# A spectral filter beside a product-key expert layer on one core: score columns laid key by key, expert flags weighted on ScalarE, and the written-out order renewed

## The chip, the cores and the metric

One core of one Trainium2 chip runs the whole kernel. The metric is the device time of one execution in microseconds (us), the median of several runs. TensorE (PE; its weight loads are shown apart as PEld), VectorE (DVE), ScalarE (ACT), GpSimd (POOL) and SyncE (SP, which here only starts DMAs) run beside each other and wait for each other through semaphores.

## The reference

```python
def _A_ref(x, w_r, w_i):                 # a filter in the 2-D Fourier domain
    X = rfft2(x) * (w_r + 1j * w_i)      # x: 1 x 2048 x 576
    return irfft2(X, s=(2048, 576))

def _B_ref(x, w_q, k1, k2, u, v):        # 32 heads, 8 + 8 keys, 64 experts, top 1
    q = einsum("nd,dhc->nhc", xf, w_q)
    s1 = einsum("nhd,ed->nhe", q[..., :128], k1)
    s2 = einsum("nhd,ed->nhe", q[..., 128:], k2)
    e = argmax(s1) * 8 + argmax(s2)      # per token and head
    act = gelu(einsum("nd,nhd->nh", xf, u[e]))
    return sum_over_heads(act * v[e])    # softmax over one candidate is 1

xn = layernorm(x)                        # no affine part
return x + _A_ref(xn, w_r, w_i) + _B_ref(xn, w_q, k1, k2, u, v)
```

## The kernel before, in words

**Filter.** `ln` and `folds` normalise 16 tiles of 128 rows and fold the 576 columns by their symmetries (sums and differences, shared between DVE and POOL). The mean is taken out in the folds: POOL makes `rr[:, 2] = -4*mean`, and a DVE scalar_tensor_tensor adds it into the even fold. `dft128` multiplies a folded tile by a 64-point transform, whose weights `Rs` ACT scales by the row's 1/sigma; ACT and DVE evict the product into `AF_`/`AB` (and `ABL`, its 33 left-over columns). For three tiles (`RTS`) the product is made in two half-height matmuls per block. `d_fwd(g)` does the transform along the columns, `s_fwd` the rest of the one along the rows, `s_mul` multiplies with the filter (DVE reads the product from PSUM as `banks`, writes `t`; POOL combines into `y`; ACT and POOL split it into two float16 halves `yh`), `s_inv(g)` transforms back (16 of them, evicted by ACT and DVE into `AB` and `ABL`). When all 16 are in, `d_inv(t)` does the last transform per tile; ACT and DVE (and POOL for the even tiles) make `qs`/`yh` and `eo`/`t` of it, multiplying by the scale `sc[:, 12]`, POOL makes `y`/`A`, and `fin(t)` multiplies by `RT`, adds the experts' part (`CAT` times `vS`) in the same PSUM tile, DVE adds x, and two DMAs write the result.

**Experts.** `fold_part` contracts the query weights (32 loads `w<-in_wq_dram` of 576 KB) with the seven key differences per side, `fold_end` and `fold_last` turn and split them into `MU`, 448 score columns that ACT and DVE write as (64 sides and heads, 7 keys), with 64 columns for u behind them. `x_t(r)` makes the two float16 halves of x transposed (`xT`): two ACT passes and one POOL subtraction each, 16 in all. `scores(r)`, r = 0 to 7, multiplies two tiles: 28 matmuls of 512 columns. ACT makes gelu, DVE the maximum `mx` over the seven keys, the flags `eq` (buffer `w`), and their product with the weights `wt`. `route(r)` reduces the weighted flags and builds the index words with a chain of DVE steps (scratch in `MT`), `combine(r)` reduces them, turns them to int32 (two tensor_scalar), masks with `fm`, multiplies by `sc[:, 9]` and the activation, and PE turns the result into `CAT`.

**Order.** The program is recorded first. `_Plan.forward` then plays the recorded operations through five engine queues with the costs of `_Plan.cost`; among those that are ready it takes the one with the lowest number in `RANK`, a table with a number for each operation. The order in which it takes them is the order in which the instructions are issued; PSUM tiles are given out in the same pass (`LIMIT`: two tiles at a time for scores, four banks for each of the kinds a, b, c). All recorded instructions carry the line of one call in `issue`, L523.

Of the kernel before, what the change touches and what calls it, by code (L numbers as in the profile page):

```python
# [196 lines left out]
)  # L197
# [1054 lines left out]
```

## Time and profile before

| | before |
|---|---|
| median of 3 runs | 222.97 us (222.16 to 223.46) |
| the profiled execution | 221.33 us, its span 219.5 us |
| granted TensorE clock | 0.995 |
| PE / PEld busy | 193.5 us (88%) / 130.7 us |
| DVE busy | 178.0 us (81%) |
| ACT / POOL busy | 132.5 us (60%) / 134.1 us (61%) |
| DMA | 48.12 MB |

Busy time is per engine, as a share of the span. An engine can be busy all the time in one stage and idle in another, so the stages are looked at one by one below. The profiled execution is 1.83 us longer than its span and 1.64 us under the median.

### The profile page before, as it was taken

To read this page: it belongs to the slowest core of one execution; us is meant where nothing else is said; L and a number is where in the kernel's file an instruction comes from. 1 tells how busy PE (TensorE), PEld (TensorE's weight loads), DVE (VectorE), ACT (ScalarE), POOL (GpSimd) and SP (SyncE) were. 2 spreads that over 40 slices of the span, in tenths; PEclk is the share of its full clock that TensorE was granted. 3 is DMA by queue.
4 is the path that set the end of the run, shared out by engine and by line. 5 is a ranking of instruction groups with operands and counts; after the bars stand their busy time and mean duration, and the time that the engine had idled before them with its cause. 6 is when DMAs were issued, how large, how long until landed. Compare 5 with 4: busy or idle time off the path is not lost.

```text
span 219.5 us, 6058 instructions
## 1 busy us (share of the span) xinstructions
PE 193.5 (88%) x2360; PEld 130.7 (60%) x2360; DVE 178.0 (81%) x417; ACT 132.5 (60%) x285; POOL 134.1 (61%) x179
## 2 busy tenths in 40 slices
PE   0197899999999989999989999999979999998690
PEld 0175576679568546764657545655547787477560
DVE  1989899854646777763999999998899999999980
ACT  2268787979946977988595983855832333043220
POOL 4776787515189307394767963947734985667560
PEclk9999999999999999999999999999999999999998
DMA  6999999999999999993362404201100136204376
GB/s 198 380 417 418 422 418 423 395 403 400 366 383 356 405 408 423 437 345 133 103 199 63 131 0 122 73 3 24 39 0 3 28 87 162 54 0 108 96 176 165
DMA packets 17020, 48.12 MB, mean 219 GB/s; under 512 B 2144, under 2 KB 8544, under 8 KB 16224
## 3 DMA queue, kind: packets, MB, share of 16 engines
q1 hardware_dynamic: 16992, 47.74, 60.6%
q8 instruction: 18, 0.29, 0.5%
q14 instruction: 10, 0.08, 0.1%
HBM read 43.01 MB, written 4.72 MB: 217 GB/s over the span
## 4 chain that ended last, share of the span: by engine, by line
PE 50%; DVE 33%; ACT 6%; issue 5%; DMA 2%; POOL 1%; ACTq 0%; DVEq 0%; POOLq 0%
PE banks L523 50%; DVE MT L523 8%; DVE t L523 7%; DVE w L523 5%; DVE XN L523 3%; DVE AB L523 2%; DVE mx L523 2%; DVE st L523 2%; DMA XN<-in_x_dram 2%; DVE A L523 2%; DVE ABL L523 2%; ACT t L523 1%; ACT ABL L523 1%; ACT AB L523 1%; ACT Rs L523 1%
## 5 line engine op out<-in xcount | busy, mean ns | idle before, releaser
L523 PE MATMUL banks<-MU,xT 128*128 128x512 f16 x192 | 45.5, 379 | 0.4 <-DVE t L523 0.4
L523 POOL TENSOR_TENSOR A<-t 128x145 f32<-128x145 f32 (+2 forms) x48 | 32.3, 688 | 14.1 <-DVE t L523 11.6
L523 PE MATMUL banks<-c,AB 128*128 128x145 f16 (+2 forms) x320 | 38.2, 253 | 1.0 <-DVE AB L523 1.0
L523 POOL TENSOR_TENSOR y<-t,t 128x289 f32<-128x289 f32 x32 | 23.0, 742 | 20.9 <-DVE t L523 20.5
L523 PEld LDWEIGHTS <-xT 128*128 128x128 f16 x224 | 20.9, 98 | 23.9 <-issue 0.9
L523 POOL TENSOR_TENSOR xT<-xf,xT 128x640 f16<-128x640 f32 x16 | 22.4, 1403 | 18.2 <-ACT xf L523 18.1
L523 DVE SCALAR_TENSOR_TENSOR t<-banks,wx,Wt 128x578 f32<-128x578 f32 x32 | 24.4, 810 | 4.1 <-PE banks L523 4.0
L523 ACT ACTIVATE yh<-banks,sc 128x580 f32<-128x580 f32 (+1 forms) x16 | 10.0, 627 | 25.1 <-PE banks L523 24.0
L523 POOL TENSOR_TENSOR yh<-y,yh 128x578 f16<-128x578 f32 x16 | 21.8, 1377 | 4.7 <-issue 2.7
L523 ACT ACTIVATE AB<-banks 128x512 f32<-128x512 f32 (+1 forms) x32 | 18.7, 592 | 5.5 <-PE banks L523 2.9
L523 PE MATMUL banks<-Rs,yl 128*99 128x128 f32 (+1 forms) x76 | 10.3, 290 | 12.6 <-ACT Rs L523 12.1
L523 PE MATMUL banks<-w,KP 128*32 128x288 f32 x256 | 20.4, 420 | 0.6 <-DMA w<-in_wq_dram 0.4
L523 PE MATMUL banks<-c,ABL 99*128 99x289 f16 (+1 forms) x64 | 18.6, 295 | 2.4 <-DVE XN L523 1.4
L523 DVE TENSOR_TENSOR ABL<-banks,ABL 33x256 f16<-33x256 f32 x32 | 12.9, 407 | 8.8 <-ACT ABL L523 6.2
L523 POOL TENSOR_TENSOR t<-XN 128x289 f32<-128x289 f32 x20 | 15.8, 799 | 5.3 <-DMA XN<-in_x_dram 2.5
L523 PEld LDWEIGHTS banks<-c,AB 128*128 128x128 f32 x128 | 18.0, 191 | 1.5 <-DVE AB L523 0.9
L523 PEld LDWEIGHTS <-AB 128*128 128x128 f16 x192 | 17.2, 146 | 2.5 <-issue 1.6
L523 PE MATMUL banks<-Rs,A 128*128 128x128 f32 (+1 forms) x152 | 18.0, 291 | 0.4 <-ACT Rs L523 0.4
L523 DVE TENSOR_REDUCE MT<-w 128x128 bf16<-128x896 bf16 (+1 forms) x16 | 18.3, 1141 | 0.1
L523 PEld LDWEIGHTS banks<-Rs,A 128*128 128x128 f32 (+1 forms) x152 | 16.8, 205 | 2.0 <-ACT Rs L523 1.0
L523 PE MATMUL banks<-A,s 64*64 64x289 f32 x256 | 17.8, 410 | 0.0
L523 PEld LDWEIGHTS banks<-Rs,yl 128*99 128x99 f32 (+1 forms) x76 | 8.1, 177 | 15.8 <-ACT Rs L523 13.5
(126 smaller groups left out, 409.1 us busy)
## 6 DMA issues: line engine op xcount, KB each, us to landing
w<-in_wq_dram SPq DMA_DIRECT2D x32, 576.0 KB, 7.4
xf<-in_xT_dram SPq DMA_DIRECT2D x16, 320.0 KB, 3.9
Wt<-in_W_dram SPq DMA_DIRECT2D x8, 578.0 KB, 6.9
out_dram<-XN SPq DMA_DIRECT2D x32, 144.0 KB, 2.4
XN<-in_x_dram SPq DMA_DIRECT2D x3, 1154.0 KB, 10.2
s<-in_s_dram SPq DMA_DIRECT2D x16, 192.0 KB, 4.2
XN<-in_xd_dram SPq DMA_DIRECT2D x2, 1152.0 KB, 8.9
XN<-in_xd_dram SPq DMA_DIRECT2D x1, 2304.0 KB, 12.9
```

What stands on the lines that cost most here:

```text
L523: fn(*[x.place() if isinstance(x, _Ps) else x for x in args], **{k: x.place() if isinstance(x, _Ps) else x for k, x in kw.items()})
```

## The change

- **Layout.** The score columns go from (64, 7 keys) to (7 keys, 64): `fold_end` and `fold_last` read PSUM in steps and write densely, the maximum over keys and the reduction of the flags read with a step of 64 elements. `fold_last` makes its low half in four DVE instructions for one.
- **Flags.** For rounds r = 0 to 6 the product with `wt` (one DVE tensor_tensor of 128x896) becomes seven ACT copies with a constant scale, 128x2x64 each. Round 7 keeps the product.
- **Index words.** The two int32 conversions of each `combine` go from DVE to ACT.
- **Scales.** `sc[:, 9]` is multiplied into `cst` once, `sc[:, 12]` into `RT` once; so the scalar_tensor_tensor of `combine` and those of `d_inv` become tensor_tensor, and ACT's copies in `d_inv` lose their pointer operand.
- **Mean.** The zero-frequency rows of the constant `C1` are set to zero; `rr[:, 2]` and its five POOL instructions go, and the even fold becomes a tensor_tensor.
- **Folds.** One of the two short folds goes from POOL to DVE for the eight even tiles (`DF`).
- **Splits.** For six of the 16 x tiles (`XL` = 4 to 9) the second ACT pass and POOL's subtraction become one DVE scalar_tensor_tensor of 128x640.
- **RTS** goes: all 16 tiles use full-height matmuls.
- **gelu_table.** One small Gelu activation behind `x_scale` asks for the table before the first scores.
- **Order.** Some costs of the planner and the whole table `RANK` are new.

Instructions by engine, counted from the two programs: DVE 419 to 415, ACT 269 to 329, POOL 184 to 165, SP 120 and 120; on PE 36 half-height matmuls become 18 full-height ones.

```diff
 RANK = (
-    1200, 1203, 1204, 1217, 1230, 1244, 1205, 1236, 588, 595, 828, 589, 1117, 799, 1029, 1035, 319, 1118, 965,
+    1212, 1222, 1221, 1226, 1282, 1283, 1225, 1223, 1150, 875, 1179, 1018, 399, 915, 971, 942, 1066, 380, 438,
...
+    C1[:, ll == 0] = 0.0
...
-        G.tensor_scalar(rr[:, 2, t:t + n], m, -4.0, None, op0=OP.mult)
...
+    def gelu_table():
+        plan.extra = 1283.0
+        A.activation(bx[:, 4:5], bx[:, 2:3], AF.Gelu_apprx_tanh)
+        plan.extra = 0.0
...
-    RTS = (9,10,11,)
+    DF = (0,2,4,6,8,10,12,14,)
...
-        G.tensor_tensor(F[:, 1, 0:145], e[:, 1, 0:145], e[:, 1, 288:143:-1], op=OP.add)
-        V.scalar_tensor_tensor(F[:, 0, 0:145], e[:, 0, 0:145], rr[:, 2, t:t + 1], e[:, 0, 288:143:-1],
-                               op0=OP.add, op1=OP.add)
+        (V if t in DF else G).tensor_tensor(F[:, 1, 0:145], e[:, 1, 0:145], e[:, 1, 288:143:-1], op=OP.add)
+        V.tensor_tensor(F[:, 0, 0:145], e[:, 0, 0:145], e[:, 0, 288:143:-1], op=OP.add)
...
+        V.tensor_scalar(cst, cst, sc[:, 9:10], None, op0=OP.mult)
...
+        V.tensor_scalar(RT, RT, sc[:, 12:13], None, op0=OP.mult)
...
-        m = (MU[:, :, c] if c < 4 else MUL)[:, :, :336].rearrange("p h (m e) -> p h m e", e=7)
-        parted(m[:, 0], m[:, 1], p.rearrange("p b m e -> p (b m) e")[:, :, :7], 0, 128 if c < 4 else 64)
+        m = (MU[:, :, c] if c < 4 else MUL)[:, :, :448].rearrange("p h (e m) -> p h e m", m=64)[:, :, :, 0:48]
+        parted(m[:, 0], m[:, 1], p.rearrange("p b m e -> p e (b m)")[:, :7], 0, 128 if c < 4 else 64)
...
+            if 2 * r + i in XL:
+                V.scalar_tensor_tensor(v, w, bx[:, 3:4], h, op0=OP.mult, op1=OP.subtract)
+                continue
...
-        V.tensor_reduce(mx, sv, axis=AX, op=OP.max)
+        V.tensor_reduce(mx, sv.rearrange("p t e m -> p t m e"), axis=AX, op=OP.max)
...
-        V.tensor_tensor(wk[:, 896:1792].rearrange("p (t n) -> p t n", t=2), wk[:, 0:896].rearrange("p (t n) -> p t n", t=2),
-                        wt.unsqueeze(1).to_broadcast([128, 2, 448]), op=OP.mult)
+        if r in AW:
+            for e in range(7):
+                A.activation(we[:, :, e], eq[:, :, e], AF.Copy, scale=2.0 ** -(6 * e + 6 + 6 * (e > 2)))
+        else:
+            V.tensor_tensor(we, eq, wt.unsqueeze(1).to_broadcast([128, 2, 7, 64]), op=OP.mult)
...
-            V.tensor_scalar(ci[:, :, w], cw[:, w].rearrange("p t i -> p (t i)"), 2.0 ** (18 + 30 * w), None, op0=OP.mult)
+            A.activation(ci[:, :, w], cw[:, w].rearrange("p t i -> p (t i)"), AF.Copy, scale=2.0 ** (18 + 30 * w))
...
-        V.scalar_tensor_tensor(ca, ct.rearrange("p (t a) k -> p t (a k)", t=2), sc[:, 9:10], act, op0=OP.mult, op1=OP.mult)
+        V.tensor_tensor(ca, ct.rearrange("p (t a) k -> p t (a k)", t=2), act, op=OP.mult)
...
-        V.scalar_tensor_tensor(eo[:, :, 0:145], p[:, :, 0:145], sc[:, 12:13], qs, op0=OP.mult, op1=OP.add)
+        V.tensor_tensor(eo[:, :, 0:145], p[:, :, 0:145], qs, op=OP.add)
```

What the new order moves is shown at three places. First PE, where the first score matmul stands. Before, these rows come just ahead of it (`yl` is the operand of an `s_inv`, the sixth of them; `c_72` and `AB` are a `d_fwd`):

```order
L523 LDWEIGHTS yl_106
L523 MATMUL banks<-s_0_115,yl_106 99x128
L523 MATMUL banks<-c_68,xT_93 128x128
L523 MATMUL banks<-c_72,AB 128x144
L523 MATMUL banks<-c_72,AB 128x145
L523 LDWEIGHTS xT_94
L523 MATMUL banks<-MU,xT_94 128x512
```

After the change the same place reads:

```order
L529 MATMUL banks<-c_72,AB 128x144
L529 LDWEIGHTS ABL
L529 MATMUL banks<-c_72,ABL 128x289
L529 MATMUL banks<-c_72,AB 128x145
L529 LDWEIGHTS xT_94
L529 MATMUL banks<-MU,xT_94 128x512
```

Six `s_inv` stand ahead of the first score matmul before, four after; the `d_fwd` and `s_fwd` ahead of it are the same number (12 and 4 pairs).

Second, ACT around the first gelu (`MT<-banks,gs`), before:

```order
L523 ACT_TABLE_LOAD
L523 ACTIVATE MT<-banks,gs 128x64
L523 ACTIVATE yl_106<-yh_133 128x396
L523 ACTIVATE xT_94<-xf_124,bx 128x640
L523 ACTIVATE yl_107<-yh_134 128x396
L523 ACTIVATE xf_124<-xf_124,bx 128x640
L523 ACTIVATE MT<-banks,gs 128x64
```

and after, from the second gelu of the first round on (`w_121<-w_121` and `w_122<-w_122` are weighted flags):

```order
L529 ACTIVATE AB<-banks 128x8x64
L529 ACTIVATE w_121<-w_121 128x2x64 x3
L529 ACTIVATE yl_106<-yh_133 128x396
L529 ACTIVATE w_121<-w_121 128x2x64 x3
L529 ACTIVATE yl_107<-yh_134 128x396
L529 ACTIVATE w_121<-w_121 128x2x64
L529 ACTIVATE xT_95<-xf_126,bx 128x640
L529 ACTIVATE MT<-banks,gs 128x64
L529 ACTIVATE ABL<-banks 99x4x64
L529 ACTIVATE MT<-banks,gs 128x64
L529 ACTIVATE xT_95<-xf_124,bx 128x640
L529 ACTIVATE w_122<-w_122 128x2x64 x7
```

The table load now stands some 80 rows earlier, behind `bx`; the flags of round 0 are cut into 3, 3 and 1 by other work, those of round 1 stand seven in a row.

Third, DVE from the last eviction of `AB` (the end of `s_inv`) on. Before:

```order
L523 TENSOR_TENSOR AB<-banks,AB 128x8x64
L523 TENSOR_TENSOR w_121<-w_121,wt 128x896
L523 TENSOR_TENSOR w_119<-w_119,MT 128x512
L523 TENSOR_REDUCE MT<-w_119 128x32
L523 SCALAR_TENSOR_TENSOR MT<-mx_127,MT 128x128
L523 TENSOR_SCALAR MT<-MT 128x16
L523 SCALAR_TENSOR_TENSOR t_0_98<-banks,sc,yh_133 128x2x145
L523 TENSOR_REDUCE MT<-w_121 128x128
```

After:

```order
L529 TENSOR_TENSOR AB<-banks,AB 128x8x64 x2
L529 TENSOR_TENSOR w_121<-w_121,MT 128x512
L529 TENSOR_REDUCE MT<-w_122 128x128
L529 TENSOR_TENSOR MT<-MT,fm 128x128
L529 SCALAR_TENSOR_TENSOR MT<-mx_129,MT 128x128
L529 TENSOR_TENSOR MT<-MT 128x128
L529 SCALAR_TENSOR_TENSOR MT<-MT 128x64
L529 TENSOR_TENSOR w_122<-MT,iv 128x512
L529 TENSOR_REDUCE MT<-w_121 128x32
```

At this place six rounds of scores and one `combine` are through PE before, seven and three after. Behind it DVE still has two `mx`, two flag comparisons, three products with `wt`, five reductions of 128x32 and ten int32 conversions before; one, one, one, three and none after.

More of the change, by code (lines that the diff above doesn't have):

```diff
@@ L308, in cost @@
                 return max(n, 128) / 2.4 * (2 if ins[0].dtype == F32 else 1) + 4, 230.0
-            c = max(n, 64) / 2.4 + (2.5 if n > 256 else 5) if ins[0].dtype != F32 else max(n, 128) * 4 / 2.4 + 8
+            c = max(n, 64) / 2.4 + (2.5 if n > 256 or n < 100 else 7) if ins[0].dtype != F32 else max(n, 128) * 4 / 2.4 + 8
             if kw.get("tile_position"):
                 q = _parts(ins[0])
-                return c * q[0] * q[1] / 16384, 230.0
+                return c * q[0] * q[1] / 16384 * (0.935 if q == [64, 128] else 1.037), 230.0
             return c, 230.0
         if eng == "scalar":
-            return (95 if ins[0].space == PSUM else 130) + 0.75 * n + 80 * ptr + 270 * ("accum_out" in kw), 180.0
+            a = 92 + 0.765 * n if ins[0].space == PSUM else 118 + 0.8 * n
+            return a + 80 * ptr + 110 * ("accum_out" in kw), 180.0
         if eng == "gpsimd":
             if m == "tensor_tensor":
-                return 60 + n * (2.25 if size_of(ins[0].dtype) + size_of(ins[1].dtype) == 8 else 2.05), 75.0
+                return (60 if n > 128 else 125) + n * (2.25 if size_of(ins[0].dtype) + size_of(ins[1].dtype) == 8 else 2.05), 75.0
             return 45 + 1.15 * n, 75.0
@@ L335, in add @@
         c, lat = self.cost(eng, m, out, ins, kw)
+        c += self.extra
         sb = [x for x in ins if x.space != PSUM and int(np.prod(x.shape[1:])) > 1]
@@ L692, in ln @@
         V.scalar_tensor_tensor(r, q, 96.0, r, op0=OP.add, op1=OP.mult)
-    bx = K([128, 4], F32, "bx")
+    bx = K([128, 5], F32, "bx")
     gs = K([128, 16], F32, "gs")
@@ L733, in dft128 @@
         p = PS("x")
-        hi = AF_.rearrange("p c (h n) -> p (c h) n", n=64)[:, :, 4 * t:4 * t + 4]
-        lo = ABL[:99].rearrange("p b (h n) -> p (b h) n", n=64)[:, :, 4 * t:4 * t + 4]
-        if t in RTS:
-            for k in range(6):
-                for h in range(2):
-                    hs = slice(64 * h, 64 * h + 64)
-                    w = F[hs, k // 2, 161 * (k % 2):161 * (k % 2) + 128] if k < 4 else FL[hs, k - 4].rearrange("p a b -> p (a b)")
-                    o = p[:, h, 64 * k:64 * k + 64] if k < 4 else p[:99, h, 64 * k:64 * k + 64].rearrange("p (q i x) -> p i q x", i=2, x=4)
-                    r = Rs[hs].rearrange("p (k h c) -> p h k c", h=2, c=2)[:, h]
-                    P.matmul(o, w, r, start=True, stop=True, tile_position=(64 * h, 0))
-            hi, lo = (v.rearrange("p k (h c) -> p k h c", h=2) for v in (hi, lo))
-            m = p[:, :, 0:256].rearrange("p h (k c) -> p k h c", c=2)
-            l = p[:99, :, 256:384].rearrange("p h (k c) -> p k h c", c=2)
-            A.activation(hi, m, AF.Copy)
-            A.activation(lo, l, AF.Copy)
-            V.tensor_tensor(lo[:33], l[:33], lo[:33], op=OP.subtract)
-            return
         m = p[:, 0].rearrange("p (h e) -> p h e", e=4)
@@ L758, in dft128 @@
             P.matmul(p[:99, 1, 128 * b:128 * b + 128].rearrange("p (q i x) -> p i q x", i=2, x=8), FL[:, b, :, :].rearrange("p a b -> p (a b)"), Rs, start=True, stop=True)
-        A.activation(hi, m, AF.Copy)
+        A.activation(AF_.rearrange("p c (h n) -> p (c h) n", n=64)[:, :, 4 * t:4 * t + 4], m, AF.Copy)
+        lo = ABL[:99].rearrange("p b (h n) -> p (b h) n", n=64)[:, :, 4 * t:4 * t + 4]
         A.activation(lo, l, AF.Copy)
@@ L895, in fold_last @@
             turned(p[:, c], c, 3)
-        m = MU[:, :, :, 336:448].rearrange("p h c (m e) -> p h c m e", e=7)
-        parted(m[:, 0], m[:, 1], p[:, :, :, :7], 1)
+        m = MU[:, :, :, :448].rearrange("p h c (e m) -> p h c e m", m=64)[:, :, :, :, 48:64]
+        q = p.rearrange("p c m e -> p c e m")[:, :, :7]
+        A.activation(m[:, 0], q, AF.Copy, scale=sc[:, 7:8])
+        for c in range(4):
+            V.scalar_tensor_tensor(m[:, 1, c], q[:, c], sc[:, 7:8], m[:, 0, c], op0=OP.mult, op1=OP.subtract)
         p = PS("m", (128, 16, 8))
         turned(p, 4, 3)
-        m = MUL[:, :, 336:448].rearrange("p h (m e) -> p h m e", e=7)
-        parted(m[:, 0], m[:, 1], p[:, :, :7], 1, 64)
+        m = MUL[:, :, :448].rearrange("p h (e m) -> p h e m", m=64)[:, :, :, 48:64]
+        parted(m[:, 0], m[:, 1], p.rearrange("p m e -> p e m")[:, :7], 1, 64)
     XT, gate = {}, set()
+    XL = (4,5,6,7,8,9,)
     @staged
@@ L914, in x_t @@
             A.activation(h, w, AF.Copy, scale=bx[:, 3:4])
+            v = x[:, i, 5:10].rearrange("p c n -> p (c n)")
+            if 2 * r + i in XL:
+                V.scalar_tensor_tensor(v, w, bx[:, 3:4], h, op0=OP.mult, op1=OP.subtract)
+                continue
             A.activation(w, w, AF.Copy, scale=bx[:, 3:4])
-            G.tensor_tensor(x[:, i, 5:10].rearrange("p c n -> p (c n)"), w, h, op=OP.subtract)
-    RT_ = {}
+            G.tensor_tensor(v, w, h, op=OP.subtract)
+    RT_, AW = {}, (0,1,2,3,4,5,6,)
     @staged
@@ L935, in scores @@
         G.tensor_tensor(act, act, cst.unsqueeze(1).to_broadcast([128, 2, 64]), op=OP.mult)
-        sv = p[:, :, :448].rearrange("p t (m e) -> p t m e", e=7)
+        sv = p[:, :, :448].rearrange("p t (e m) -> p t e m", m=64)
         mx = T([128, 2, 64], F32, "mx", 4)
-        V.tensor_reduce(mx, sv, axis=AX, op=OP.max)
+        V.tensor_reduce(mx, sv.rearrange("p t e m -> p t m e"), axis=AX, op=OP.max)
         wk = T([128, 2304], BF, "wk", 5, "w")
-        eq = wk[:, 0:896].rearrange("p (t m e) -> p t m e", t=2, e=7)
-        V.tensor_tensor(eq, sv, mx.unsqueeze(3).to_broadcast([128, 2, 64, 7]), op=OP.is_equal)
-        V.tensor_tensor(wk[:, 896:1792].rearrange("p (t n) -> p t n", t=2), wk[:, 0:896].rearrange("p (t n) -> p t n", t=2),
-                        wt.unsqueeze(1).to_broadcast([128, 2, 448]), op=OP.mult)
+        eq, we = (wk[:, 896 * k:896 * k + 896].rearrange("p (t e m) -> p t e m", t=2, e=7) for k in range(2))
+        V.tensor_tensor(eq, sv, mx.unsqueeze(2).to_broadcast([128, 2, 7, 64]), op=OP.is_equal)
+        if r in AW:
[3 more added lines that the diff above has]
+            V.tensor_tensor(we, eq, wt.unsqueeze(1).to_broadcast([128, 2, 7, 64]), op=OP.mult)
         RT_[r] = (act, mx, wk)
@@ L948, in route @@
         act, mx, wk = RT_.pop(r)
-        wv = wk[:, 896:1792].rearrange("p (m e) -> p m e", e=7)
+        wv = wk[:, 896:1792].rearrange("p (t e m) -> p t m e", t=2, e=7)
         O1 = wk[:, 1792:2304].rearrange("p (t i h) -> p t i h", t=2, i=8)
@@ L952, in route @@
         v0 = view(RM[:, 0:64], [128, 128], BF)
-        V.tensor_reduce(v0, wv, axis=AX, op=OP.max)
+        V.tensor_reduce(v0.rearrange("p (t m) -> p t m", t=2), wv, axis=AX, op=OP.max)
         vf = view(RM[:, 64:128], [128, 2, 2, 32], BF)
@@ L1099, in d_inv @@
             es = T([128, 2, 290], F32, "qs", 2, "yh")
-            A.activation(es, p[:, :, 0:290], AF.Copy, scale=sc[:, 12:13])
+            A.activation(es, p[:, :, 0:290], AF.Copy)
             qs = es[:, :, 145:290]
@@ L1145, in _body @@
     x_scale()
+    gelu_table()
     gate.add(len(plan.ops) - 1)
     plan.gate = gate
-    wt = K([128, 448], BF, "wt")
-    V.tensor_copy(wt.rearrange("p (m e) -> p m e", e=7), mk[:, 20:27].unsqueeze(1).to_broadcast([128, 64, 7]))
+    wt = K([128, 7, 64], BF, "wt")
+    V.tensor_copy(wt, mk[:, 20:27].unsqueeze(2).to_broadcast([128, 7, 64]))
     iv = K([128, 8, 32], BF, "iv")
```

14 lines of the change are left out of this document (6 added, 8 removed), and 125 rows, old and new, of the table RANK.

## The prediction

> **What bounds the kernel now.** I read the page's busy shares and chain first, then busy time by stage, then the timeline where one stage passes into the next. The page says:
>
> ```profile
> PE 193.5 (88%) x2360; PEld 130.7 (60%) x2360; DVE 178.0 (81%) x417; ACT 132.5 (60%) x285; POOL 134.1 (61%) x179
> PE 50%; DVE 33%; ACT 6%; issue 5%; DMA 2%; POOL 1%; ACTq 0%; DVEq 0%; POOLq 0%
> ```
>
> PE is the main load, and a third of the chain that ended last is DVE. The stages, cut at the first matmul (9.95), at the first score matmul (95.9), at the end of the last `s_inv` (160.0) and at PE's last matmul (213.65); columns are the stretch, its length, then busy time of PE, PEld, DVE, ACT and POOL:
>
> ```profile
> 9.95:95.90 85.95, 81.39 (x992) 59.53 (x993) 64.42 (x190) 67.68 (x157) 49.56 (x69) 1.00 1.02 405
> 95.90:160.00 64.10, 63.25 (x714) 36.27 (x711) 55.04 (x104) 45.56 (x87) 43.76 (x45) 1.00 0.29 90
> 160.00:213.65 53.65, 48.85 (x660) 34.92 (x656) 52.35 (x102) 16.54 (x38) 35.29 (x50) 1.00 0.30 71
> 213.65:219.50 5.85, 0.00 (x0) 0.00 (x0) 0.82 (x1) 0.00 (x0) 0.00 (x0) 0.83 0.72 171
> ```
>
> Until 160 PE is hardly ever idle (4.6 us of 86, 0.9 of 64). In the last stage DVE is busy 52.35 of 53.65 us: there DVE is the bound. How much PE work that stage holds I price from the timeline, since a busy PE may still be stretched:
>
> ```profile
> 160.01 2.76 PE L523 MATMUL banks<-MU,xT 128*128 128x512 f16 x12
> ...
> 171.56 0.29 PE L523 MATMUL banks<-c,ABL 99*128 99x290 f16 x1
> ...
> 172.08 0.29 PE L523 MATMUL banks<-c,ABL 99*128 99x290 f16 x1
> ...
> 197.35 0.67 PE L523 MATMUL banks<-A,c 64*64 64x288 f32 x8
> ...
> 198.20 0.67 PE L523 MATMUL banks<-A,c 64*64 64x288 f32 x8
> ...
> 207.56 0.40 PE L523 MATMUL banks<-id,CZ 128*128 128x64 f16 x8
> ```
>
> Twelve score matmuls take 2.76, so the 28 of a round 6.45; half a `d_inv` is 172.08 - 171.56 = 0.52, so one is 1.04; a `fin` is 198.20 - 197.35 = 0.85; a `combine` is put at 0.35, a little under its row because its end overlaps. Left at 160 are 2 rounds, 16 `d_inv`, 16 `fin`, 7 `combine`: 12.9 + 16.6 + 13.6 + 2.5 = 45.6 us of work in 53.65. So the last stage has **8 us of slack on PE**, and the first two stages have next to none.
>
> **The change, part by part: DVE.** Rows with counts, busy time and mean of one:
>
> ```profile
> L523 DVE TENSOR_TENSOR w<-w,wt 128x896 bf16<-128x896 bf16 x8 | 5.4, 671 | 0.0
> L523 DVE TENSOR_SCALAR MT<-MT 128x16 int32<-128x16 f32 x16 | 4.3, 295 | 0.0
> L523 DVE SCALAR_TENSOR_TENSOR MT<-MT,sc 128x128 f32<-128x128 int32 x8 | 3.7, 462 | 0.0
> L523 DVE TENSOR_TENSOR MT<-MT,fm 128x128 int32<-128x128 int32 x8 | 2.5, 311 | 0.0
> L523 DVE SCALAR_TENSOR_TENSOR t<-banks,sc,yh 128x290 f32<-128x290 f32 x16 | 8.1, 506 | 0.0
> L523 DVE SCALAR_TENSOR_TENSOR t<-banks,wx,Wt 128x578 f32<-128x578 f32 x32 | 24.4, 810 | 4.1 <-PE banks L523 4.0
> L523 DVE TENSOR_TENSOR AB<-banks,AB 128x512 f16<-128x512 f32 x16 | 10.8, 678 | 2.0 <-ACT AB L523 2.0
> L523 DVE SCALAR_TENSOR_TENSOR vS<-Wt,sc,vS 128x576 f16<-128x576 f32 x1 | 0.8, 819 | 0.3 <-ACT vS L523 0.3
> L523 DVE SCALAR_TENSOR_TENSOR A<-t,rr 128x145 f32<-128x145 f32 x16 | 7.1, 448 | 0.9 <-POOL t L523 0.7
> L523 DVE TENSOR_TENSOR A<-t 128x288 f32<-128x288 f32 x16 | 7.2, 448 | 0.0
> L523 POOL TENSOR_TENSOR A<-t 128x145 f32<-128x145 f32 x16 | 8.5, 535 | 6.3 <-DVE t L523 4.1 <-PE banks L523 1.0 <-ACT Rs L523 0.9
> ```
>
> - Flags: seven products go, 7 x 0.671 = 4.7. Index words: all sixteen, 4.3.
> - The `combine` product without pointer: nearest row the masking of the same size, 0.311 for 0.462, so 8 x 0.15 = 1.2; at worst nothing.
> - `d_inv`: 578 elements with a pointer take 0.810, 512 without 0.678; 66 more at DVE's 1.04 ns an element (a slope estimated from the 145 and 288 column rows below 0.31 and 0.448) make 0.747, so the pointer costs 0.06: 24 x 0.06 = 1.4, with 0 and 0.1 each as ends.
> - Splits: the row of `vS` has the same form at 576; 640 make 0.886, six of them +5.3, three of which stand behind the first `mx` in the new order, +2.7.
> - Folds: 145 elements without pointer, between nothing saved (0.448) and the 288-column row less 143 elements (0.30); I take 0.31. Then 16 x 0.14 saved pays for eight more folds, net 0. POOL loses 8 x 0.535, and the mean's five.
>
> From the first `mx` to the end that is 4.7 + 4.3 + 1.2 + 1.4 - 2.7 = **8.9 us less DVE work**. For the last stage I count the new order's DVE rows behind the last evictions (two of everything becomes one, five reductions three, ten conversions none) at the means of that stage: 58.7 before, 42.7 after. The first sum is measured as 52.35, as overlapping instructions are counted twice, so the second is worth 38 less one us: 37.
>
> **PE.** Its work is the same but for `RTS` and changes of tile shape:
>
> ```profile
> 27.64 1.12 PE L523 MATMUL banks<-Rs,yl 128*99 128x128 f32 x8
> ...
> 30.47 0.69 PE L523 MATMUL banks<-w,KP 128*32 128x288 f32 x8
> 31.61 1.11 PE L523 MATMUL banks<-Rs,A 64*128 64x64 f32 x16 [0.44 <-ACT Rs L523]
> ...
> 33.00 0.69 PE L523 MATMUL banks<-w,KP 128*32 128x288 f32 x8
> 33.62 0.68 PE L523 MATMUL banks<-Rs,yl 128*99 128x128 f32 x4
> 34.23 1.18 PE L523 MATMUL banks<-w,KP 128*32 128x288 f32 x16
> 35.34 2.20 PE L523 MATMUL banks<-Rs,A 128*128 128x128 f32 x24
> ```
>
> Two full tiles run from 27.64 to 30.47, 1.42 each; the half-height one from 31.61 to 33.00, 1.39: no difference. Eight key matmuls take 0.62 start to start, sixteen 1.11, so a group carries 0.13 that is no matmul. The new PE order has 101 changes of shape for 91: between 0.6 and 1.3, I take +1.0, all ahead of the last stage.
>
> **ACT.** The added copies are priced by their nearest rows:
>
> ```profile
> L523 ACT ACTIVATE CZ<-MT 128x128 f16<-128x128 f32 x8 | 2.5, 308 | 5.6 <-DVE MT L523 5.6
> L523 ACT ACTIVATE Rs<-c,rr 128x128 f32<-128x128 f32 x16 | 5.9, 392 | 0.4 <-DVE rr L523 0.3
> L523 ACT ACTIVATE bx<-bx 128x1 f32<-128x1 f32 x1 | 0.2, 192 | 0.0
> L523 ACT ACTIVATE xf<-xf,bx 128x640 f32<-128x640 f32 x16 | 13.2, 823 | 0.2
> ...
> 9.21 0.69 ACT L523 ACTIVATE Rs<-c,rr 128x128 f32<-128x128 f32 x2 [0.27 <-DVE rr L523]
> ```
>
> A flag copy is 0.308 alone; two `Rs` of 0.392 take 0.69, so a follower can save 0.09. Seven take 1.6 to 2.2, and 49 take 11 to 15. Sixteen conversions at 0.21 (between 0.192 and 0.308) are 3.4; six `xf` fewer save 4.9. Between first scores and last `s_inv` ACT holds 45.56 before; 46 flags, eight conversions, one more round and two more `s_inv` (about 1.1 for both evictions and 1.2 for `yh` and `yl` each, estimated by size from the `xf` row) less four `xf` bring it to about 61 to 65 in some 73 us. It fits, by throughput. The table load moves into the first stage, where ACT is busy 67.68 of 85.95:
>
> ```profile
> 99.58 1.28 ACT L523 ACT_TABLE_LOAD   x1
> 100.87 0.31 ACT L523 ACTIVATE MT<-banks,gs 128x64 f32<-128x64 f32 x1
> ```
>
> I count +0.4 for it and for the slower first rows (bounds 0 and 1.3). The Trainium skill, "ScalarE: Activation LUTs", section "What ACT_TABLE_LOAD costs", puts a switch of sets at about 2.66 us with a drain behind the load. This trace shows gelu 1.29 after the load's start and no drain; by the page the moved load would cost at most 1.4 more.
>
> **The sum.** The first score starts two `s_inv` earlier, which then follow it, so they cancel. The end of the last `s_inv` moves from 160.0 by one round more ahead of it (+6.45), two combines (+0.7), shapes (+1.0), the early load (+0.4) and 0.6 more idle, as DVE and ACT are fuller there: 169.2. Behind it PE has one round, 16 `d_inv`, 16 `fin`, five `combine`: 6.45 + 16.6 + 13.6 + 1.75 = 38.4 us, DVE 37. Two engines that are equally loaded and wait for each other don't run without loss; I take half of today's 8 us, 4.0. PE then ends at 211.6 for 213.65, a gain of **2.0**, and I add 0.3 for POOL, which is 16 us lighter in the first stages. The tail of 5.85 (last addition, queue of output DMAs) stays: four additions in a row end both orders. So 221.33 - 2.3 = 219.0 for the profiled execution, which lay 1.64 under the median of 222.97: **220.7 us** for the median. About 0.5% (1.1 us) is what a measurement of this kernel can tell from no change.
>
> **The rivals.**
> - *More is won.* The last stage runs at DVE's 37 to PE's 38.4 with 1 us lost, and the first stage loses half of its 4.6 us idle as POOL is relieved: 2.3 + 3 + 2 less 1.3 for shapes, 217. For it: DVE alone fills that stage today. Against: every `fin` hangs on ACT, DVE and POOL in turn.
> - *No gain: slack stays.* 6 us of loss instead of 4 in the last stage eat the gain: 222.7. DVE's relief then does nothing, as its place is taken by the chain of a tile.
> - *No gain: steps in memory.* The maximum and the reduction of the flags now read every 64th element. The one stepped DVE read in the trace, one of two reductions of 288, costs nothing (447 and 458 ns), but PE's weight loads do slow down on stepped tiles (146 for 98):
>
> ```profile
> L523 DVE TENSOR_REDUCE mm__96<-banks x2: 447/452/458, 85.4 to 88.0; 128x1 f32<-128x288 f32 x2
> ...
> L523 PEld LDWEIGHTS <-xT 128*128 128x128 f16 x224 | 20.9, 98 | 23.9 <-issue 0.9
> L523 PEld LDWEIGHTS <-AB 128*128 128x128 f16 x192 | 17.2, 146 | 2.5 <-issue 1.6
> ```
>
>  By that ratio sixteen reductions of 1.08 grow by 0.53, 8.5 us, which cancels the relief: about 223. "SBUF — State Buffer", Door 1, in the Trainium skill has the rule: reads that leave a 16-byte line of SBUF (8 in PSUM) at each access pay a penalty. The 447 and 458 speak against it for PSUM; no row shows a stepped bf16 read.
> - *Slower: evictions behind flags.* ACT works in order. Seven flags in a row hold it 1.6 to 2.2 us; PE covers about 1.05 (one `s_inv`) with the two tiles it may have open. If most of the seven groups stand ahead of an eviction PE needs, each costs 0.55 to 1.1, together 3.9 to 7.7: 1.6 to 5.4 slower, 224.6 to 228.4. It decides as soon as PE waits for ACT over 0.3 us per group. For it: round 1's seven in one piece. Against: other rounds are cut into threes and fours with evictions between.
>
> **How the numbers follow.** Forecast 0.40 (219.2 to 221.8), more 0.22, no gain 0.19 (steps 0.09, slack 0.10), slower 0.19. Faster 0.62, within 0.5% 0.19, slower 0.19. The range leaves out a tenth at each end: from 216.5, the better end of the second case, to 225.2, the near part of the slow one.
>
> **What would show it.** Right: first score matmul within 2 us of 95.9; last `s_inv` near 169; DVE about 172 us busy in all, ACT 142 to 147, POOL near 118; in the last stage some 42 us, DVE under 92% busy. A flag copy near 0.31 and `mx` near 1.08. Wrong: `mx` or the flag reduction over 1.3 (steps), PE waiting for ACT more than 5 us between 95 and 170 (flags), or a last stage over 45 us (slack).

## The result, and the profile after

The changed kernel takes **229.87 us** (median of 4 runs, 229.78 to 229.96) where the kernel before took 222.56 beside it: 1.0328 times as long, 95% interval 1.0283 to 1.0373. I had forecast 220.7 and a range up to 225.2; it is 7.3 us slower, not 2.3 faster. The profiled execution took 229.82 us, its span 228.0. All medians and ratios below are of fast executions; one slow one of a_tree, 394.13 us, is left out.

The page of the changed kernel, busy time and the chain that ended last:

```profile
PE 196.3 (86%) x2324; PEld 132.1 (58%) x2324; DVE 186.9 (82%) x413; ACT 137.0 (60%) x345; POOL 116.9 (51%) x160
DVE 48%; PE 28%; ACT 12%; issue 6%; DMA 2%; POOL 2%; POOLq 0%; DVEq 0%; ACTq 0%
```

DVE was to get lighter and is 8.9 us busier; on the chain PE and DVE have changed places (PE had 50%, DVE 33%). By stage, cut at the same events (first matmul, first score matmul, end of the last `s_inv`, PE's last matmul; columns as before):

```profile
10.09:97.21 87.12, 80.90 (x885) 58.69 (x886) 67.29 (x199) 65.82 (x154) 40.46 (x53) 0.98 1.00 394
97.21:177.51 80.30, 73.11 (x830) 41.88 (x828) 72.09 (x120) 53.47 (x144) 40.96 (x46) 1.00 0.24 75
177.51:222.05 44.54, 42.01 (x612) 31.55 (x612) 41.08 (x73) 14.93 (x44) 30.21 (x46) 1.00 0.35 85
```

The middle stage is where the time went: 80.3 us. PE is idle in 7.2 of them (80.30 - 73.11), 0.85 before (64.10 - 63.25), while DVE is busy 90%. By releaser its waits there add up to 7.0: 4.2 for DVE (1.3 each for `ABL` and for `w`), 2.0 for ACT and 0.8 for POOL. The rows of DVE and ACT that the change touches:

```profile
L529 DVE TENSOR_REDUCE MT<-w 128x128 bf16<-128x896 bf16 x8 | 13.9, 1734 | 1.2 <-ACT w L529 1.2
L529 DVE TENSOR_REDUCE mx<-banks 128x128 f32<-128x896 f32 x8 | 8.6, 1078 | 0.4 <-PE banks L529 0.4
L529 DVE SCALAR_TENSOR_TENSOR xT<-xf,bx,xT 128x640 f16<-128x640 f32 x6 | 5.3, 885 | 1.1 <-ACT xT L529 1.1
L529 DVE TENSOR_TENSOR MT<-MT 128x128 f32<-128x128 int32 x8 | 4.4, 548 | 0.0
L529 DVE TENSOR_TENSOR A<-t 128x145 f32<-128x145 f32 x24 | 8.4, 367 | 0.6 <-PE banks L529 0.6
L529 DVE TENSOR_TENSOR t<-banks,yh 128x290 f32<-128x290 f32 x16 | 7.2, 450 | 2.4 <-ACT yh L529 2.3
L529 DVE TENSOR_SCALAR c<-c,sc 128x64 f32<-128x64 f32 x1 | 0.7, 677 | 0.0
L529 ACT ACTIVATE w<-w 128x128 bf16<-128x128 bf16 x49 | 11.7, 306 | 4.3 <-DVE w L529 4.3
```

The reduction of the weighted flags took 1.073 before and takes 1.734: reading bf16 in SBUF with a step of 64 elements costs 0.66 us each, 5.3 in all. The maximum `mx`, which reads fp32 in PSUM with the same step, takes 1.078 where it took 1.081: no cost. The flag copy (0.306), the split (0.885) and `d_inv` (0.450) are as forecast.

A stretch of the middle stage shows how such a microsecond reaches PE. DVE's timeline, then POOL's and PE's:

```profile
134.39 1.71 DVE L529 TENSOR_REDUCE MT<-w 128x128 bf16<-128x896 bf16 x1
136.01 0.28 DVE L529 TENSOR_TENSOR MT<-MT,fm 128x128 int32<-128x128 int32 x1
136.21 0.28 DVE L529 SCALAR_TENSOR_TENSOR MT<-mx,MT 128x128 bf16<-128x128 f32 x1
136.41 1.49 DVE L529 TENSOR_TENSOR MT<-MT 128x128 f32<-128x128 int32 x1
137.82 0.41 DVE L529 TENSOR_TENSOR w<-MT,iv 128x512 bf16<-128x512 bf16 x1
138.16 0.21 DVE L529 SCALAR_TENSOR_TENSOR MT<-MT 128x64 bf16<-128x64 bf16 x1
138.29 0.74 DVE L529 TENSOR_TENSOR ABL<-banks,ABL 33x256 f16<-33x256 f32 x2
```
```profile
136.28 1.47 POOL L529 TENSOR_TENSOR xT<-xf,xT 128x640 f16<-128x640 f32 x1 [1.62 <-ACT xf L529]
```
```profile
136.72 0.70 PE L529 MATMUL banks<-A,s 64*64 64x289 f32 x2
138.75 1.45 PE L529 MATMUL banks<-A,s 64*64 64x289 f32 x20 [1.34 <-DVE ABL L529]
```

PE waits 1.34 us for an eviction (`ABL`) that stands in DVE's queue behind the stepped reduction and behind a product that takes 1.49. The same product takes 0.27 at its fastest. Its row and that of an int32 conversion of the kernel before (minimum, median, maximum in ns):

```profile
L529 DVE TENSOR_TENSOR MT<-MT x8: 269/308/1486, 133.5 to 214.2; 128x128 f32<-128x128 int32 x8
```
```profile
L523 DVE TENSOR_SCALAR MT<-MT x16: 156/164/1266, 123.8 to 206.5; 128x16 int32<-128x16 f32 x16
```

The slow product began 0.13 us after POOL's subtraction and ended 0.15 after it: **DVE waited for POOL, and the profile books the wait as busy**. The Trainium skill, "SBUF — State Buffer", section "Who interferes with whom", has the rule: a DVE instruction with two SBUF inputs and a GpSimd one that reads SBUF exclude each other for the whole instruction. This trace agrees: of its 56 two-input rows of `route` and `combine`, 14 took over 0.1 us more than the fastest of their kind. All 14 began while a POOL instruction ran, and each ended a fixed time after it (0.15 us for the rows of 128 elements, 0.08 for 64, 0.28 for 512). Together they lost 8.1 us. The conversion of 1.266, which has one SBUF input, ended 0.03 after POOL as well, so a second input is not needed for such a wait.

### The profile page after: what moved, and what is told of

The parts are those of the page before. It is cut to its first block, busy times and chain, and to the rows that moved or that the text cites. A ratio compares the mean times of both kernels' runs of the same rounds, so it can differ in the third digit from the quotient of the medians.

```text
span 228.0 us, 6021 instructions
## 1 busy us (share of the span) xinstructions
PE 196.3 (86%) x2324; PEld 132.1 (58%) x2324; DVE 186.9 (82%) x413; ACT 137.0 (60%) x345; POOL 116.9 (51%) x160
## 4 chain that ended last, share of the span: by engine, by line
DVE 48%; PE 28%; ACT 12%; issue 6%; DMA 2%; POOL 2%; POOLq 0%; DVEq 0%; ACTq 0%
PE banks L529 28%; DVE MT L529 11%; DVE t L529 10%; DVE w L529 5%; DVE st L529 4%; DVE A L529 4%; DVE mx L529 3%; DVE ABL L529 3%; DVE XN L529 2%; ACT w L529 2%; DVE AB L529 2%; ACT AB L529 2%; DMA XN<-in_x_dram 2%; ACT yh L529 1%; ACT yl L529 1%
## 5 line engine op out<-in xcount | busy, mean ns | idle before, releaser
L529 POOL TENSOR_TENSOR y<-t,t 128x289 f32<-128x289 f32 x32 | 23.7, 764 | 28.0 <-DVE t L529 26.3
L529 POOL TENSOR_TENSOR A<-t 128x289 f32<-128x289 f32 (+2 forms) x40 | 25.9, 664 | 8.3 <-DVE t L529 6.6
L529 PE MATMUL banks<-Rs,yl 128*99 128x128 f32 x64 | 11.4, 318 | 15.7 <-ACT Rs L529 13.7
L529 DVE TENSOR_REDUCE MT<-w 128x128 bf16<-128x896 bf16 (+1 forms) x16 | 23.5, 1470 | 1.2 <-ACT w L529 1.2
L529 POOL TENSOR_TENSOR xT<-xf,xT 128x640 f16<-128x640 f32 x10 | 14.3, 1436 | 17.6 <-ACT xf L529 17.6
L529 POOL TENSOR_TENSOR yh<-y,yh 128x578 f16<-128x578 f32 x16 | 20.4, 1288 | 5.6 <-ACT yh L529 3.2
L529 PEld LDWEIGHTS banks<-Rs,yl 128*99 128x99 f32 x64 | 9.1, 193 | 17.9 <-ACT Rs L529 14.4
L529 PE MATMUL banks<-Rs,A 128*128 128x128 f32 x128 | 19.0, 302 | 0.0
L529 PEld LDWEIGHTS banks<-Rs,A 128*128 128x128 f32 x128 | 17.7, 216 | 1.9 <-issue 1.9
L529 ACT ACTIVATE yh<-banks 128x290 f32<-128x290 f32 (+1 forms) x16 | 8.4, 531 | 15.8 <-PE banks L529 12.1
```

The lines of the kernel that those rows point to most:

```text
L529: fn(*[x.place() if isinstance(x, _Ps) else x for x in args], **{k: x.place() if isinstance(x, _Ps) else x for k, x in kw.items()})
```

## The experiments

Each keeps the instruction order of the kernel it starts from, row for row; an instruction more stands right behind the one that was recorded ahead of it. Names with a_ start from the changed kernel, with b_ from the one before. Theory 1: the edits add DVE work and DVE ends the middle stage. Theory 2: the renewed order is to blame. Theory 3: ACT's queue is. Ratios are to the kernel before, run beside them, and gains and losses of b_ runs in us are worked out from them.

Small differences need the granted clock beside them. The 77 executions of the kernel before that ran beside the experiments fall into two kinds: 39 with a granted clock of 0.992 to 0.997, median 221.9 us, and 38 with 0.976 to 0.990, median 223.3. Every profiled execution with a clock of 0.990 or less has a stretch of about 3.4 or 6.8 us, sometimes several, in which PE gets half its clock while it still has work; in that of the changed kernel the granted clock is 0.50 from 18.1 to 21.4 us. No profiled execution with a higher clock has one. All four executions of the changed kernel are of the second kind. "At equal clock" below compares medians of one kind among executions that ran beside each other. This sorting was made afterwards and some groups are small, so it shows where a small difference may come from and proves none.

**All edits in the old order (b_ops)**, all but RTS, planner costs and RANK.

> The kernel before in its own order, with all edits of the change made in place (layout, ACT flags, index words, scales, mean, folds, splits, early gelu table), all but RTS, the planner's costs and the order. Theory 1 (the edits are to blame, they add 8 to 9 us of DVE work): 226 to 231. Theory 2 (the order is to blame): 219 to 223.

229.49 us, ratio 1.0322 (1.0273 to 1.0372): the same loss as the whole change. Theory 2 falls: the edits cost it, and the new order neither adds nor returns anything that can be measured. The reduction takes 1.75 there too.

**Dense reduction, paid by ACT (a_dense).**

```diff
-        eq, we = (wk[:, 896 * k:896 * k + 896].rearrange("p (t e m) -> p t e m", t=2, e=7) for k in range(2))
+        eq = wk[:, 0:896].rearrange("p (t e m) -> p t e m", t=2, e=7)
+        we = wk[:, 896:1792].rearrange("p (t m e) -> p t e m", t=2, e=7)
```

> The changed kernel, its order of instructions kept row for row; ACT writes the weighted flags key by key for each side, so that DVE's reduction of them reads dense again. Theory 1 (the change added DVE work, and DVE ends the middle stage): the reduction goes from 1.73 to about 1.07 us, DVE falls by 5.3 us, the time by 3.5 to 5.3, to 224.6 to 226.4. Theory 2 (the new order and the flags in ACT's queue hold PE up): the time stays within 1 us of 229.9, or rises, as ACT's copies now write in steps (0.31 to perhaps 0.45 us each, 7 us in all).

240.42 us, ratio 1.0818 (1.0767 to 1.087). DVE lost what was forecast (the reduction is back at 1.084), but writing bf16 in steps of 14 bytes is far dearer than I had put it, on ACT and, in round 7, on DVE:

```profile
L538 ACT ACTIVATE w<-w 128x128 bf16<-128x128 bf16 x49 | 27.7, 873 | 6.1 <-DVE w L538 6.1
...
L538 DVE TENSOR_TENSOR w<-w,wt 128x896 bf16<-128x896 bf16 x1 | 4.1, 4137 | 0.0
```

So it doesn't test theory 1 cleanly: 16 us more in ACT's flag copies, with ACT busy only 63%, went with 10.6 us more time, though DVE was 4.2 lighter.

**Flags, index words and scale in the old layout (b_relief).** ACT copies `we[:, :, :, e]` from `eq[:, :, :, e]`, so both sides step; `combine` and `d_inv` as in the change, with `sc[:, 9]` kept.

> The kernel before in its own order and old layout, with only the edits that really take work from DVE: flags of rounds 0 to 6 weighted by seven ACT copies, index words on ACT, the inverse scale in RT and so no pointer in d_inv. DVE should lose 4.7 + 4.3 + 1.4 = about 10 us, ACT gets 12 to 20. Theory 1: faster than before, 216 to 220, since DVE alone fills the last stage. Theory 2 (ACT works in order, and seven flags ahead of an eviction hold PE): 223 to 228.

239.28 us, 1.0756 (1.0669 to 1.0842): the same trap, a copy takes 0.919. DVE is 6.3 us lighter (171.7) and the kernel 17 slower.

**Splits back to ACT and POOL (a_split)**: `XL` empty.

> The changed kernel in its own order; the six splits of x tiles go back from DVE to one more ACT pass and a POOL subtraction each (POOL's stands right behind where ACT's is issued). DVE loses 6 x 0.89 = 5.3 us, ACT gets 4.9, POOL 8.5. Theory 1: all six stand between 96 and 125 us where DVE is now the bound, so 3 to 5 us are won, 225 to 227. Theory 2: nothing won, 229 to 232, since ACT's queue gets longer.

233.99 us, 1.0525 (1.0467 to 1.0584). DVE's busy time fell by 4.3 us (186.9 to 182.6), ACT's rose by 4.5 and POOL's by 7.2, and the kernel is 4 slower, more than either theory gave. In this order the splits on DVE pay; in the old one they cost 1.3 (b_xl, below).

**Flags back on DVE (a_flagsdve)**: one product of 128x896 for the seven copies.

> The changed kernel in its own order and layout, with the flags of all rounds weighted by one DVE product, put where the first of the seven ACT copies stood. DVE gets 7 x 0.61 to 1.04 = 4.3 to 7.3 us, ACT loses 11.7. Theory 1 (DVE's work sets the end of the middle stage): 4 to 7 slower, 234 to 237. Theory 3 (ACT's queue does: copies that stand ahead of evictions and reads in its order): 2 to 5 faster, 225 to 228.

233.0 us (231.47 to 234.14), 1.045 (1.0363 to 1.0536). Theory 3 expected faster and falls as the sole cause; theory 1 has the sign, with 3 for its 4 to 7 (the interval just touches that of the change).

**Layout alone in the old order (b_layout_dve, b_layout_act)**: with one DVE product per round, and with ACT's copies.

> The kernel before in its order with the new layout alone; flags stay one DVE product per round. The stepped reduction grows from 1.07 to 1.74 us, 5.4 in all. Theory 1: 4 to 6 slower than before, 226 to 228. Theory 3: at most 2 slower, as ACT's queue is what it was.

225.87 us, 1.0121 (1.0026 to 1.0215).

> The same as b_layout_dve, but rounds 0 to 6 weighted by seven ACT copies of 0.31. DVE loses 7 x 0.61 = 4.3 us against it, ACT gets 10.5. Theory 1: 3 to 4 faster than b_layout_dve. Theory 3: 2 to 5 slower than b_layout_dve.

227.25 us, 1.0192 (1.012 to 1.0263). The layout costs 2.7 us (its interval is 0.6 to 4.8) for 5.5 more of DVE, nearly all of it the stepped reduction (1.740). The ACT flags take 4.9 us from DVE (183.5 to 178.6) and gain nothing: the medians are 1.4 apart the other way, and the intervals overlap. At equal clock the layout costs 3.4 with DVE's product and 3.9 with ACT's copies, so the flags cost 0.5; neither theory 1 (3 to 4 faster) nor theory 3 (2 to 5 slower) gave that.

**Index words and inverse scale (b_cidinv).**

> The kernel before in its order, with the index words on ACT and the inverse scale in RT alone. DVE loses 4.3 + 1.4 us, most of it in the last stage, where DVE was busy 97.6%; ACT gets 3.4 and loses 1.5. Theory 1: 3 to 5 faster, 217 to 219. Theory 3: 1 to 3 faster, since sixteen short copies more stand in ACT's queue but the last stage's ACT is idle 70% of the time.

221.71 us, 0.9959 (0.9922 to 0.9996): 0.9 gained by the ratio, not the 3 to 5 of theory 1. Even the 0.9 is not shown: nine of its ten executions had a granted clock of 0.992 or more, but only five of the 13 of the kernel before beside it, and at equal clock the medians are 221.63 and 221.53.

**The other edits singly, in the old order: splits (b_xl), mean and folds (b_folds), early table (b_gelu).**

> The kernel before in its order; only the six splits go to DVE. DVE +5.3 us, ACT -4.9, POOL -8.4. Theory 1 (DVE's work ends the stages): 3 to 5 slower than before, 226 to 228. Theory 3 (ACT's queue does): within 1 of it, or faster.

223.96 us, 1.0059 (1.0029 to 1.009): 1.3 slower for 4.5 us more of DVE (178.0 to 182.5), 1.5 at equal clock.

> The kernel before in its order; only the mean leaves the folds (POOL -3.3 us, no pointer in sixteen DVE folds) and one fold of the eight even tiles goes from POOL to DVE. DVE gets 24 x 0.32 for 16 x 0.45, +0.3, POOL -8. All of it lies ahead of 46 us, where PE waits 4 us. Theory 1 and 3 alike: within 1 us of before, 222 to 223.5; if the first stage is held by DVE's short steps there, 1 to 2 slower.

221.58 us, 0.9956 (0.9929 to 0.9984): 1.0 faster, 0.7 to 0.9 at equal clock.

> The kernel before in its order; only the table is asked for behind the x scale. Theories 1 and 3: within 0.7 us of before; a fourth one (ACT's 1.3 us in a full first stage holds PE up) gives 1 to 1.5 slower.

223.71 us, 1.0049 (1.0023 to 1.0074): 1.1 slower, the fourth case; 1.5 at equal clock.

At equal clock these single edits add up to the loss: layout and ACT flags 3.9, splits 1.5, table 1.5, index words and inverse scale 0.1, mean and folds -0.8, together 6.2 us; b_ops, whose executions are all of the second kind, lies 6.2 above the two such executions of the kernel before beside it. By the ratios they give 1.9 + 0.6 + 0.5 - 0.4 - 0.4 = 2.2% for 3.2%. The scale in `cst` was not run singly in this order, and that the sums meet so closely is in part luck.

**PE's wait at 15 us (a_warm).**

```diff
+        if t == 2:
+            for _ in range(4):
+                P.matmul(p[:, 1, 256:384], idn, Rm, start=True, stop=True)
```

> The changed kernel in its own order, with four more fp32 matmuls of 128x128 (their product isn't used) in the place where PE waits 2.79 us from 15.2 to 18.0. If the low clock behind that wait (8 matmuls in 1.96 us where 1.12 is usual, 4.5 us for two tiles) comes from the wait, two tiles take 2.9 again and the first score comes 1.2 to 1.7 earlier, the time is 228 to 229. If it is a matter of time since the start, nothing changes: 229.9.

229.2 us, 1.028 (1.0254 to 1.0307), an interval that overlaps that of the change: inconclusive. In the profiled execution (229.87 us, granted clock 0.989) the added matmuls shortened the wait from 2.79 to 1.88 us, and the eight matmuls behind it still took 1.93. The other four executions had a granted clock of 0.994 to 0.998, which none of the changed kernel's four reached, and a median of 229.1. So the stretch at half clock is worth some 0.8 us of the 7.3 here; five executions don't show that the added matmuls remove it.

**A cheaper reduction with nothing given away (a_tree).**

```diff
-        V.tensor_reduce(v0.rearrange("p (t m) -> p t m", t=2), wv, axis=AX, op=OP.max)
+        V.tensor_tensor(we[:, :, 0:3], we[:, :, 0:3], we[:, :, 3:6], op=OP.max)
+        V.tensor_tensor(we[:, :, 0], we[:, :, 0], we[:, :, 1], op=OP.max)
+        V.tensor_tensor(we[:, :, 2], we[:, :, 2], we[:, :, 6], op=OP.max)
+        V.tensor_tensor(v0.rearrange("p (t m) -> p t m", t=2), we[:, :, 0], we[:, :, 2], op=OP.max)
```

> The changed kernel in its own order; the reduction of the weighted flags over the stepped keys (1.73 us) becomes four tensor_tensor maxima of 384, 128, 128 and 128 dense bf16 elements, estimated at 0.85 us together from the 512-element bf16 row of 0.41. Nothing is given to another engine. Theory 1 (DVE's added work lengthens the middle stage): DVE -6 to -7, the time 4 to 6 faster, 224 to 226. Theory 3 (ACT's queue alone): less than 1.5 us.

227.56 us, 1.0227 (1.0181 to 1.0273): 2.3 faster than the change by the medians, 2.2 by the ratios, and the intervals don't touch. Its middle and last stage:

```profile
97.41:176.26 78.85, 72.78 (x831) 41.89 (x829) 69.08 (x138) 53.49 (x144) 39.88 (x46) 1.00 0.25 79
176.26:219.99 43.73, 41.69 (x612) 31.24 (x612) 39.81 (x78) 15.10 (x44) 30.95 (x46) 1.00 0.37 89
```

DVE is 3.0 us lighter in the middle stage, ACT is not (53.49 for 53.47), and the stage is 1.45 shorter: half of the relief arrives, between both theories. Four maxima took 1.3 together, not 0.85: they read two SBUF inputs, and some rows wait for POOL (the last maximum takes 0.224 at its fastest and 0.616 at its slowest).

**Versions in the old order (b_best, b_tree, b_tree_dve).** b_best has the edits that gained singly by their ratios.

> The kernel before in its order with the edits that gained: mean, folds, index words on ACT, inverse scale in RT. If they add, 1.9 us faster than before, about 220.5; if they take the same slack, 221.5.

221.07 us, 0.9931 (0.9904 to 0.9958): faster than both kernels; by the ratios the two gains nearly add. At equal clock it is 0.6 faster, about what the mean and the folds gave alone.

> b_best with the new layout, the ACT flags and the four maxima in place of the stepped reduction. DVE loses 4.3 (flags) and 1.5 to 2 (reduction) against before. Theory 1: 218 to 220. Theory 3: slower than b_best by 1 to 3, as ACT's flags cost 1.4 in the old order.

225.99 us, 1.0148 (1.0104 to 1.0192).

> The same with the flags weighted by one DVE product per round. DVE loses 1.5 to 2 (reduction) against b_best and ACT 10.5 against b_tree. Theory 1: 1 to 2 faster than b_best, 2 to 3 slower than b_tree. Theory 3: faster than b_tree by 1 to 3.

225.26 us, 1.0114 (1.0072 to 1.0157). Both are 4 to 5 slower than b_best, about 3 at equal clock, so the new layout loses even with the four maxima, and again the ACT flags gain nothing.

**Which edits make the gain (b_best_comb, b_best_nodf).**

> b_best with sc[:, 9] multiplied into cst, so that the product of combine has no pointer. By b_ops (0.369 for 0.462) eight products save 0.7 us of DVE, half of it in the last stage where DVE is busy 97%: 0.3 to 0.7 faster than b_best, 220.5 to 221. If the extra 0.26 us on the scale's chain or the slower row of the changed kernel (0.548) decides, 0 to 0.7 slower.

220.44 us, 0.9913 (0.9879 to 0.9947).

> b_best_comb with the eight folds back on POOL (the mean still gone). DVE loses 8 x 0.32 = 2.5 us ahead of 46 us, POOL gets 4.3. If the folds on DVE were what gained in b_folds, 0.5 to 1 slower than b_best_comb; if the mean was, the same within 0.5.

220.94 us, 0.9921 (0.9893 to 0.995). The intervals of the three overlap: all lie 0.7 to 0.9% under the kernel before (0.3 to 0.7% at equal clock), and the folds on DVE are not what gains.

## Why the prediction was wrong

**1. "8.9 us less DVE work" (failed: the step that decides).** From the first score to PE's last matmul DVE is busy 72.09 + 41.08 = 113.2 us for 55.04 + 52.35 = 107.4: 5.8 more. Of the 14.7 between: 5.3 are the stepped reduction, which the forecast put at nothing and kept as a rival, there with a cost for `mx` too, which has none. As the rival itself says, no row showed a stepped bf16 read, so the nothing in the sum had no ground. 1.9 are `combine`'s product (+0.7 for -1.2). 1.7 are splits: five follow the first score, not three. 1.1 are the scaling of `RT`, which I did not count, and round 7's flag product, whose one row took 1.042. 2.3 are two `s_mul` products and the two evictions of one `s_inv` more that the order moved behind the first score. 2.6 are rows that nobody edited, all two-input ones, which got longer. The rest of that sum was right: `d_inv` 1.3 for 1.4, the index words 4.3. (The slope of 1.04 ns an element in the `d_inv` term doesn't come out of its two rows, which give 0.138 us over 143 elements, 0.97; with that the term would be 1.6.)

**2. "DVE is the bound" of the last stage (right as read, wrong as understood).** The 97.6% was not all work. b_best_comb shows it: it takes four kinds of rows off DVE there and puts cheaper ones in their place. Kernel before, last stage, DVE:

```profile
L523 DVE TENSOR_TENSOR w<-w,MT 128x512 bf16<-128x512 bf16 x10 | 4.6, 485 | 0.0
...
L523 DVE SCALAR_TENSOR_TENSOR MT<-MT,sc 128x128 f32<-128x128 int32 x5 | 2.7, 536 | 0.0
L523 DVE TENSOR_SCALAR MT<-MT 128x16 int32<-128x16 f32 x10 | 2.4, 263 | 0.0
L523 DVE SCALAR_TENSOR_TENSOR MT<-mx,MT 128x128 bf16<-128x128 f32 x4 | 1.7, 428 | 0.0
L523 DVE TENSOR_TENSOR MT<-MT,fm 128x128 int32<-128x128 int32 x5 | 1.7, 331 | 0.0
```

b_best_comb, the same:

```profile
L534 DVE TENSOR_TENSOR w<-w,MT 128x512 bf16<-128x512 bf16 x10 | 6.1, 638 | 0.0
...
L534 DVE TENSOR_TENSOR MT<-MT,fm 128x128 int32<-128x128 int32 x5 | 2.6, 526 | 0.0
L534 DVE SCALAR_TENSOR_TENSOR MT<-mx,MT 128x128 bf16<-128x128 f32 x4 | 2.3, 566 | 0.0
L534 DVE TENSOR_TENSOR MT<-MT 128x128 f32<-128x128 int32 x5 | 2.1, 423 | 0.0
```

The conversions' 2.4 are gone, the product saves 0.6 and `d_inv` 1.4, 4.4 together; three untouched rows grow by 1.5, 0.9 and 0.6, 3.0 together. What was taken away had partly been waiting for POOL, and the next two-input instruction now waits instead: in the whole run 18 of the 56 such rows of `route` and `combine` took over 0.1 us more than the fastest of their kind, all of them behind a POOL instruction. The stage itself, in the columns used above, did not get shorter (53.65 us and 52.35 of DVE before):

```profile
159.78:213.38 53.60, 48.78 (x656) 34.88 (x656) 51.92 (x92) 16.57 (x48) 33.54 (x50) 1.00 0.30 72
```

So DVE's share of that stage was no measure of what relief would bring. I took the mean of 0.295 for a conversion whose median is 0.164; the median is the work.

**3. The middle stage (failed).** I gave it 74 us (169.2 less a first score at 95.2), with 0.6 of new idle time. It took 80.3, with 6.3 more idle PE. The rival that named a mechanism for a loss, evictions behind ACT's flags, is not borne out alone: PE waited for ACT 2.0 us there, not over 5, and a_flagsdve took the flags from ACT and lost 3. In the old order the ACT flags gained nothing though DVE lost 4.9 us. What the runs show is that DVE, ACT and POOL wait for each other: one engine's relief arrived by half (a_tree), and the splits moved back to ACT and POOL cost more than they saved (a_split). In the old order the new layout is the largest single loss, 3.4 of 6.2 us at equal clock. How the loss splits in the new order stays open: there the splits on DVE gain 4, in the old one they cost 1.5.

**4. The last stage (42.4 forecast, 44.5 measured; the mechanism right, a size off).** It became a PE stage: DVE's share is 92% (41.08 of 44.54), PE is busy 42.01. The forecast had 38.4 of PE work and 4.0 of waiting; it was 42.0 and 2.5. PE of the changed kernel there:

```profile
198.29 0.72 PE L529 MATMUL banks<-A,c 64*64 64x288 f32 x8
198.82 0.55 PE L529 MATMUL banks<-vS,MT 64*64 64x288 f16 x12
199.30 0.34 PE L529 MATMUL banks<-c,ABL 99*128 99x290 f16 x1
199.48 0.57 PE L529 MATMUL banks<-c,AB 128*128 128x145 f16 x6
199.89 0.29 PE L529 MATMUL banks<-c,ABL 99*128 99x290 f16 x1
200.02 0.57 PE L529 MATMUL banks<-c,AB 128*128 128x145 f16 x6
200.52 0.72 PE L529 MATMUL banks<-A,c 64*64 64x288 f32 x8
```

A `fin` and a `d_inv` in turn take 200.52 - 198.29 = 2.23. I had priced them at 0.85 + 1.04 = 1.89, from stretches in which two of a kind follow each other; I put the 0.34 down to the two changes of tile shape per pair, which no run tests by itself. I counted such changes only ahead of this stage.

**5. The first stage (1.4 forecast, 3.4 measured).** The first score is 1.3 later with two `s_inv` (2.1) less ahead of it. b_gelu prices the early table at 1.1 (0.23 to 0.74%), near the bound of 1.3 and not at 0.4. The other part is the start, the changed kernel first, then the one before:

```profile
11.91 3.25 PE L529 MATMUL banks<-Rs,A 128*128 128x128 f32 x16
17.96 1.96 PE L529 MATMUL banks<-Rs,yl 128*99 128x128 f32 x8 [2.79 <-ACT Rs L529]
```
```profile
15.32 1.04 PE L523 MATMUL banks<-w,KP 128*32 128x288 f32 x8
17.55 1.12 PE L523 MATMUL banks<-Rs,yl 128*99 128x128 f32 x8 [1.19 <-ACT Rs L523]
```

The new order has no key matmuls to fill PE's wait, and the matmuls behind it take 1.96 for 1.12, with a granted clock of 0.98 over the stage for 1.00. The slower matmuls are the stretch at half clock, and that is not the new order's alone: b_ops, b_gelu and b_layout_dve have it at the same place with the key matmuls of the old order ahead of it, and the kernel before has such a clock in half of its executions, though not in the profiled one. That is why the profiled executions are 8.5 us apart and the medians 7.3. I compared this stage by its counts only.

**6. The chances.** Slower had 0.19, by a mechanism that was at most a part of it, and 229.87 lies beyond even that case's 228.4. The largest single cause found, the layout with DVE's stepped reads, stood under "no gain", because I set its cost against a relief that was itself too large.

## What to carry to other kernels

A busy engine that waits for another inside its instructions is not all work: price an instruction that you remove by its median or minimum, and look at whether the next one inherits the wait. Price a changed access pattern by its own row or keep its full cost in the forecast; here one row decided that DVE gained work where it was to lose it. When several in-order engines hand the same tile round, test edits one at a time in the unchanged order: four small ones here gave 0.8% (b_best_nodf; 0.5% at equal clock), and the large one lost more than that by itself. And compare executions of like granted clock before a gain of less than 1% is believed.
